# Half-chunk start, split last tile, and DMA transposes with GpSimd norms in a fused FFT and gated-MLP kernel

## The chip, the cores and the metric

The kernel runs on one core of one Trainium2 chip. The metric is device time in microseconds (us) of that core, one number per execution. The kernel before takes 206.59 us (median of the 3 runs that came with it, 204.63 to 207.01).

Engine names are those of the profile: PE (TensorE, matmuls), PEld (its weight loads), DVE (VectorE), ACT (ScalarE), POOL (GpSimd), SP (SyncE, which here only issues DMAs). "SPq" is the issuing of DMAs from SP. Each run has a state. For one core it is called slow when the run is over 1.5% above the fastest of the same kernel, and all ratios use fast runs.

## The reference, cut to what matters

```python
xn = _layernorm(x, axis=-1)                      # x: [1, 2048, 512] bf16
return x + _A_ref(xn, A_w_r, A_w_i) + _B_ref(xn, B_w_gate, B_w_up, B_w_down)

# _A_ref: rfft2 over (2048, 512), times a complex weight, irfft2
# _B_ref: h = gelu(xn @ w_gate) * (xn @ w_up);  h @ w_down     (512 -> 1792 -> 512)
```

## The kernel before

The 2048 rows are 16 tiles of 128, and four tiles are a chunk. Each chunk is normalised, transposed (xnT, features on partitions) and used twice. The MLP takes it in 14 blocks per chunk, each a gate and an up group of four matmuls. The FFT takes it through a "butterfly" (sums and differences) and then units D and A, whose results go out to DRAM and come back transposed as `tv`. Units B and C, a second trip through DRAM (`vv`), and units E and F follow.

Each engine gets one list of instructions, and in the traces an engine that waited at one of them stood idle (DVE for 8.52 us and PE for 8.62 us in the changed kernel). The MLP blocks fill PE, and the FFT units are placed between them by hooks: one hook after each gate, one after each up, three in each down tile. `at(h, ...)` puts work at hook h.

```python
def ln_norm(j):
    op("dve", lambda e: e.tensor_scalar(xn[:, j % 4, :], x_sb[:, j, :], ag[:, j, 0:1], rstd[:, j:j + 1], ALU.subtract, ALU.mult), ...)

def trans(m, dcs, jjs, eng="dve"):               # 8 PE transposes into one PSUM bank, then a copy
    ...
            ins = e.transpose(bank_h(bk)[:, i * P:(i + 1) * P], xn[:, jj, dc * P:(dc + 1) * P], ident[:])
    ...
        op("dve", lambda e: e.tensor_copy(dst, src), r=[("ps", bk)], w=ks)

# the plan (cut): chunks 1 to 3
for m in range(1, 4):
    a = 10 * (m - 1)
    for i in range(4):
        at(a + i, (ln_stat, 4 * m + i))
    at(a + 3, (ln_aggr, 4 * m, 4))
    for i in range(4):
        at(a + 6 + i // 2, (ln_norm, 4 * m + i))
    at(a + 8, (trans, m, (0, 1), (0, 1, 2, 3)))
    at(a + 9, (trans, m, (2, 3), (0, 1, 2, 3)))
    at(a + 10, (butter, m, 0))
    at(a + 11, (butter, m, 1))
...                                              # D of tile 4 at hook 12, of tile 8 at 22, of tile 12 at 32
for i in range(0, 16, 2):
    at(47 + 3 * i, (unit_B, i), (unit_B, i + 1)) # needs all of tv
    at(52 + 3 * i, (unit_C, i), (unit_C, i + 1))
...
# the start (cut): statistics, norms and transposes of all four tiles of chunk 0, then
for b in range(4):
    for fc in range(NFC):
        gate(b, fc); hook(False); up(b, fc); flush(); hook()
        if b > 0 and fc in (2, 5, 8, 11):
            down(b - 1, (fc - 2) // 3)
for jj in range(4):
    down(3, jj)
```

Loads of x, constants and the gate and up weights go out on the SP queue at the start, in order of need. The down weights (wd) and the FFT's weights (Wr, Wi, cm) are issued from POOL at hooks.

## Time and profile before

| what | value | read from |
|---|---|---|
| span of the profiled execution | 205.1 us | the page |
| PE busy | 190.8 us, 93% | the page, part 1 |
| first MLP matmul | 10.69 us | timeline |
| PE idle for tv ahead of the first unit B | 3.85 us | waits, timeline |
| PE idle ahead of transposes, for norms | 1.9 us in 5 waits | waits |
| last DVE add to the end | 201.37 to 205.1 us | timeline |

Three parts of the page follow, cut. First the busy times by engine (busy us, share of the span, instructions). Then the busy tenths of PE in 40 slices of 5.1 us, the granted clock (the share of the full TensorE clock that the chip let PE have) in tenths, and the DMA engines' busy share.

```profile
PE 190.8 (93%) x1131; PEld 93.2 (45%) x1145; DVE 112.1 (55%) x262; ACT 88.3 (43%) x157; POOL 25.9 (13%) x52
...
PE   7898989899999569999999999989999999999992
...
PEclk9999999999999957999999999999999999999999
DMA  5999998626675601556654223230011111111102
```

PE is the engine to look at. Its one large hole lies near 72 us, and the granted clock falls there (0.50 from 72.5 to 79.3 us). The DMA engines are at nine tenths or more from 5 to 31 us.

The chain of waits, in order of time (start us, us, what), shows that hole:

```profile
62.80 4.18 DMA scr<-tt
66.98 0.02 issue
67.00 6.27 DMA tv<-scr
73.27 0.24 issue
73.51 1.07 PE ps L455 x8
74.58 1.82 PE ps L576 x4
```

The last store of unit A and the last reload of tv take 10.5 us together. PE has MLP work for only part of that. After the hole, the four gate matmuls of one block take 1.82 us; elsewhere they take 0.86.

The waits of PE (engine, line, for whom: us in total, times, longest):

```profile
PE ps L455 <- DMA tv<-scr: 3.9, 1, 3.9
PE ps L366 <- DVE xn L356: 1.9, 5, 0.7
PE ps L406 <- DVE arena L392: 1.2, 2, 0.7
```

L366 are the transposes, and L406 is the first matmul of unit D, which waits for the butterfly on DVE.

### The profile page before, as it was taken

How to read it: one execution, taken by the hardware profiler on the slowest of the kernel's cores; microseconds unless marked ns; L12 is line 12 of the kernel's file. 1: busy time of each engine (PE TensorE's matmuls, PEld its weight loads, DVE VectorE, ACT ScalarE, POOL GpSimd, SP SyncE). 2: the span in 40 equal slices, each digit the busy share in tenths (PEclk: the TensorE clock that was granted, in tenths of full speed). 3: DMA queues.
4: the chain of work that ended last, by engine and by line, in shares of the span. 5: the costliest groups of instructions: out<-in, count | busy, mean ns of one | idle time of the engine just before them, and what ended most of it. 6: DMA issues, size and time to landing. Idle time of an engine off the chain costs nothing.

```text
span 205.1 us, 3107 instructions
## 1 busy us (share of the span) xinstructions
PE 190.8 (93%) x1131; PEld 93.2 (45%) x1145; DVE 112.1 (55%) x262; ACT 88.3 (43%) x157; POOL 25.9 (13%) x52
## 2 busy tenths in 40 slices
PE   7898989899999569999999999989999999999992
PEld 3344544445544223444444444435555555555540
DVE  2897786978422233546773677233555454546341
ACT  2135565554553131563545534414636363635210
POOL 0201125031201202222310000000100001010000
PEclk9999999999999957999999999999999999999999
DMA  5999998626675601556654223230011111111102
GB/s 147 221 312 348 281 316 185 197 79 150 107 180 148 120 18 54 113 131 134 157 162 118 62 77 106 69 87 1 16 46 44 36 33 50 39 27 29 26 26 51
DMA packets 19007, 23.09 MB, mean 113 GB/s; under 512 B 2208, under 2 KB 16672, under 8 KB 18608
## 3 DMA queue, kind: packets, MB, share of 16 engines
q1 hardware_dynamic: 16512, 16.79, 30.4%
q0 software_dynamic: 1712, 5.32, 11.8%
q10 hardware_dynamic: 768, 0.79, 1.6%
q8 instruction: 9, 0.15, 0.3%
q14 instruction: 6, 0.05, 0.1%
HBM read 16.57 MB, written 6.31 MB: 112 GB/s over the span
## 4 chain that ended last, share of the span: by engine, by line
PE 73%; DMA 10%; DVE 10%; issue 2%; POOL 1%; ACT 1%; SPq 0%
PE ps L602 20%; PE ps L589 20%; PE ps L576 19%; DMA tv<-scr 3%; DVE hT L592 3%; DVE st L344 3%; PE ps L455 2%; PE ps L481 2%; DMA scr<-tt 2%; DMA scr<-vp 2%; PE ps L515 2%; DMA x_sb<-in_A_x_dram 2%; DMA arena<-scr 2%; DVE xn L356 2%; PE ps L366 1%
## 5 line engine op out<-in xcount | busy, mean ns | idle before, releaser
L592 DVE TENSOR_TENSOR hT<-ps,gl 128x512 bf16<-128x512 f32 x56 | 38.5, 690 | 41.8 <-PE ps L589 36.8
L576 PE MATMUL ps<-xnT,wg 128*128 128x512 f16 x224 | 59.2, 388 | 0.8 <-ACT xnT L378 0.8
L589 PE MATMUL ps<-xnT,wu 128*128 128x512 f16 x224 | 58.4, 384 | 0.0
L579 ACT ACTIVATE gl<-ps 128x512 bf16<-128x512 f32 x56 | 33.4, 597 | 48.1 <-PE ps L576 44.9
L602 PE MATMUL ps<-wd,hT 128*128 128x512 bf16 x210 | 49.8, 379 | 0.8 <-issue 0.2
L576 PEld LDWEIGHTS ps<-xnT,wg 128*128 128x128 bf16 x224 | 21.0, 99 | 24.5 <-issue 4.8
L602 PEld LDWEIGHTS ps<-wd,hT 128*128 128x128 bf16 x224 | 21.3, 98 | 23.2 <-issue 1.0
L589 PEld LDWEIGHTS ps<-xnT,wu 128*128 128x128 bf16 x224 | 21.3, 99 | 22.2 <-issue 2.6
L523 POOL COPY zt<-xn 1x128 bf16<-1x128 bf16 x16 | 4.5, 283 | 79.4 <-ACT zt L522 79.4
L615 DVE TENSOR_TENSOR x_sb<-ps,x_sb 128x512 bf16<-128x512 f32 x11 | 7.6, 690 | 12.0 <-PE ps L602 12.0
L522 ACT ACTIVATE zt<-ps 128x512 bf16<-128x512 f32 x16 | 9.5, 595 | 10.5 <-PE ps L515 10.5
L549 ACT ACTIVATE eo<-ps 128x512 bf16<-128x512 f32 x16 | 9.5, 595 | 9.4 <-PE ps L544 9.4
L487 ACT ACTIVATE vp<-ps 128x514 bf16<-128x514 f32 x16 | 8.7, 598 | 10.1 <-PE ps L481 10.1
L344 DVE BATCH_NORM_STATS2 st<-x_sb 128x6 f32<-128x512 bf16 x16 | 10.6, 685 | 3.6 <-DMA x_sb<-in_A_x_dram 3.6
L413 ACT ACTIVATE xs<-ps 128x512 f16<-128x512 f32 x16 | 9.5, 596 | 6.7 <-PE ps L409 6.6
L461 ACT ACTIVATE xc<-ps 128x514 f16<-128x514 f32 x16 | 8.7, 600 | 6.9 <-PE ps L455 6.9
L440 ACT ACTIVATE tt<-ps 128x514 f16<-128x514 f32 x16 | 8.7, 598 | 3.7 <-PE ps L434 3.1
L554 DVE TENSOR_TENSOR ys<-eo 128x256 bf16<-128x256 bf16 x16 | 4.6, 289 | 9.3 <-ACT eo L549 9.3
L455 PE MATMUL ps<-tv,be 128*64 128x257 f16 x64 | 5.5, 297 | 3.9 <-DMA tv<-scr 3.9
L467 DVE TENSOR_TENSOR m_0<-xc,Wr 128x514 bf16<-128x514 f16 x8 | 3.4, 430 | 10.3 <-ACT xc L461 10.3
L352 POOL TENSOR_TENSOR rstd<-vpe,mhalf 128x4 f32<-128x4 f32 (+1 forms) x5 | 4.6, 918 | 26.6 <-DVE vpe L351 26.6
L338 PE MATMUL ps<-dumm 128*128 128x512 f16 x24 | 6.8, 454 | 1.2 <-DVE dumm L309 1.2
(65 smaller groups left out, 167.2 us busy)
## 6 DMA issues: line engine op xcount, KB each, us to landing
scr<-tt SPq DMA_DIRECT2D x16, 128.5 KB
tv<-scr SPq DMA_DIRECT2D x16, 128.5 KB
scr<-vp SPq DMA_DIRECT2D x16, 128.5 KB
arena<-scr SPq DMA_DIRECT2D x16, 128.5 KB
out_dram<-osb SPq DMA_DIRECT2D x32, 64.0 KB
wg<-in_B_w_gate_dram SPq DMA_DIRECT2D x3, 512.0 KB, 11.2
wu<-in_B_w_up_dram SPq DMA_DIRECT2D x3, 512.0 KB, 13.0
x_sb<-in_A_x_dram SPq DMA_DIRECT2D x5, 256.0 KB, 11.4
```

Source lines behind the costliest of these rows:

```text
L344: op("dve", lambda e: e.bn_stats(st[:, j, :], x_sb[:, j, :]), r=[("x", j, 0), ("x", j, 1)], w=[("st", j)])
L413: op("act", lambda e: e.activation(x4[:].rearrange("p (a c r) -> p a c r", a=2, r=4), bank(bk).rearrange("p (a r c) -> p a c r", a=2, r=4) ...
L440: op("act", lambda e: e.activation(t4[:], pair(bk), ACT.Copy, scale=SC_A), r=[("ps", bk), ("ps", bk + 1)], w=[("tt", j % 4)])
L455: ins = e.matmul(bank(bk + ri)[64 * hh:64 * hh + 64, 0:257], be[:, 64 * ri:64 * ri + 64], tv[:, 16 * hh + h, :], start=True, stop=True, sk ...
L461: op("act", lambda e: e.activation(xc[s2][:, :, 0:KD], pair(bk), ACT.Copy, scale=SC_B), r=[("ps", bk), ("ps", bk + 1)], w=[("xc", s2)])
L522: op("act", lambda e: e.activation(z[:], bank(bk).rearrange("p (a c) -> p a c", a=4), ACT.Copy, scale=SC_E), r=[("ps", bk)], w=[zk])
L549: op("act", lambda e: e.activation(o2[:], bank(bk), ACT.Copy), r=[("ps", bk)], w=[ok])
L576: ins = e.matmul(bank(bg), wg_sb[:, dc, fc * P:(fc + 1) * P], xnT[:, dc, b * 512:(b + 1) * 512], start=(dc == 0), stop=(dc == 3))
L579: op("act", lambda e: e.activation(gl[k % 2][:], bank(bg), ACT.Gelu_apprx_tanh), r=[("ps", bg)], w=[("gl", k % 2)])
L589: ins = e.matmul(bank(bu), wu_sb[:, dc, fc * P:(fc + 1) * P], xnT[:, dc, b * 512:(b + 1) * 512], start=(dc == 0), stop=(dc == 3))
L592: op("dve", lambda e: e.tensor_tensor(hT[b % 2][:, fc, :], bank(bu), gl[k % 2][:], ALU.mult), r=[("ps", bu), ("gl", k % 2)], w=[("hT", b % ...
L602: ins = e.matmul(bank(bk), hT[b % 2][:, fc, jj * P:(jj + 1) * P], wd_sb[:, fc, :], start=(fc == 0), stop=(fc == NFC - 1))
```

## The change

The change has three intents. The first three MLP blocks start on the first half of chunk 0, so that PE begins earlier. The last down tile is finished in two column halves, to shorten the tail. For chunks 1 to 3, the PE transposes and their DVE copies become one DMA transpose each, and half of their norms move to POOL, to relieve PE and DVE. Hooks shift by a few places, there are three gelu buffers and four `zt` buffers, and xnT has another layout. The core of the diff, cut:

```diff
-        load_w(wg_sb, wgv, "wg", 0, 2, "act")
-        load_w(wu_sb, wuv, "wu", 0, 2, "sp")
+        load_w(wg_sb, wgv, "wg", 0, 3, "act")
+        load_w(wu_sb, wuv, "wu", 0, 3, "sp")
 ...
         def ln_norm(j):
-            op("dve", lambda e: e.tensor_scalar(xn[:, j % 4, :], ...
+            eng = "pool" if j >= 4 and j % 2 else "dve"
+            op(eng, lambda e: e.tensor_scalar(xn[:, j % 4, :], ...
 ...
+        def trans_dma(m):
+            op("sp", lambda e: e.dma_start_transpose(xnT[:, 4 * m:4 * m + 4].rearrange("p j a c -> p (j a) c"), xn[:].rearrange("p j d -> p (j d)")),
+               r=[("xn", jj) for jj in range(4)], w=[("xnT", m, dc, jj) for dc in range(4) for jj in range(4)], dma=True)
 ...
+        def last_down(bk):          # two halves of 256 columns, each added and stored by itself,
+            ...                     # its two stores issued from sp and act
 ...
-            a = 10 * (m - 1)
+            a = 9 * (m - 1) + 3
 ...
-                at(a + 6 + i // 2, (ln_norm, 4 * m + i))
-            at(a + 8, (trans, m, (0, 1), (0, 1, 2, 3)))
-            at(a + 9, (trans, m, (2, 3), (0, 1, 2, 3)))
-            at(a + 10, (butter, m, 0))
-            at(a + 11, (butter, m, 1))
+                at(a + 5 + i // 2, (ln_norm, 4 * m + i))
+            at(a + 7, (trans_dma, m))
+            at(a + 11, (butter, m, 0))
+            at(a + 12, (butter, m, 1))
 ...                                # D of tile 4 now at hook 17, of tile 8 at 26, of tile 12 at 35
-            at(47 + 3 * i, (unit_B, i), (unit_B, i + 1))
+            at(49 + 3 * i, (unit_B, i), (unit_B, i + 1))
 ...
+        for fc in range(2):         # before the second half of chunk 0 is transposed
+            gate(0, fc, (0, 1))
+            up(0, fc, (0, 1), fc == 1)
 ...
+        gate(0, 2, (0, 1))
+        up(0, 2, (0, 1))
+                jjs = (2, 3) if b == 0 and fc < 3 else (0, 1, 2, 3)
```

More of the change, by code (lines that the diff above doesn't have):

```diff
@@ L228, in bass_parallel_sum__spectral_gfnet__glu_gated_geglu__prompt_kernel @@
         xn = sb("xn", [P, 4, D], F16)
-        xnT = sb("xnT", [P, 4, S], F16)
+        xnT = sb("xnT", [P, NJ, 4, P], F16)
         arena = sb("arena", [P, 9216], F16)
@@ L255, in bass_parallel_sum__spectral_gfnet__glu_gated_geglu__prompt_kernel @@
         vp = [sb("vp%d" % i, [P, 2, KD], BF16) for i in range(4)]
-        NZ = 6
+        NZ = 4
         zt = [sb("zt%d" % i, [P, 4, P], BF16) for i in range(NZ)]
@@ L259, in bass_parallel_sum__spectral_gfnet__glu_gated_geglu__prompt_kernel @@
         z256 = xn[:].rearrange("p a d -> p (a d)").bitcast(BF16)
-        gl = [sb("gl%d" % i, [P, 512], BF16) for i in range(2)]
+        gl = [sb("gl%d" % i, [P, 512], BF16) for i in range(3)]
         eo = [sb("eo%d" % i, [P, 512], BF16) for i in range(2)]
@@ L320, in bass_parallel_sum__spectral_gfnet__glu_gated_geglu__prompt_kernel @@
         dma("sp", fd[:], c_fd.ap(), w=["fd"])
-        load_w(wg_sb, wgv, "wg", 2, 6, "sp")
-        load_w(wu_sb, wuv, "wu", 2, 6, "sp")
+        load_w(wg_sb, wgv, "wg", 3, 6, "sp")
+        load_w(wu_sb, wuv, "wu", 3, 6, "sp")
         load_x(8, 4, 0, "sp")
@@ L355, in ln_norm @@
         def ln_norm(j):
-            op("dve", lambda e: e.tensor_scalar(xn[:, j % 4, :], x_sb[:, j, :], ag[:, j, 0:1], rstd[:, j:j + 1], ALU.subtract, ALU.mult),
+            eng = "pool" if j >= 4 and j % 2 else "dve"
+            op(eng, lambda e: e.tensor_scalar(xn[:, j % 4, :], x_sb[:, j, :], ag[:, j, 0:1], rstd[:, j:j + 1], ALU.subtract, ALU.mult),
                r=[("x", j, 0), ("x", j, 1), ("ag", j), ("rstd", j)], w=[("xn", j % 4)])
@@ L369, in trans @@
             w = len(jjs) * P
-            c0 = m * 512 + jjs[0] * P
             n = len(dcs)
-            dst = xnT[:, dcs[0]:dcs[0] + n, c0:c0 + w]
-            src = bank_h(bk)[:, 0:n * w].rearrange("p (a c) -> p a c", a=n)
+            j0 = 4 * m + jjs[0]
+            dst = xnT[:, j0:j0 + len(jjs), dcs[0]:dcs[0] + n, :].rearrange("p j a c -> p a j c")
+            src = bank_h(bk)[:, 0:n * w].rearrange("p (a j c) -> p a j c", a=n, j=len(jjs))
             ks = [("xnT", m, dc, jj) for dc in dcs for jj in jjs]
@@ L385, in butter, with t @@
             k = ("fold", m % 2)
-            sl = slice(m * 512, (m + 1) * 512)
+            lo, hi = (xnT[:, 4 * m:4 * m + 4, i:i + 2, :].rearrange("p j a c -> p a j c") for i in (0, 2))
+            def t(ap):
+                return ap.rearrange("p a (j c) -> p a j c", j=4)
             if part == 0:
-                op("dve", lambda e: e.tensor_tensor(ev1, xnT[:, 0:2, sl], xnT[:, 2:4, sl], ALU.add), r=xk(m), w=["ev1"])
-                op("dve", lambda e: e.tensor_tensor(f[:, 2:4, :], xnT[:, 0:2, sl], xnT[:, 2:4, sl], ALU.subtract), r=xk(m), w=[k + (2,), k + (3,)])
+                op("dve", lambda e: e.tensor_tensor(t(ev1), lo, hi, ALU.add), r=xk(m), w=["ev1"])
+                op("dve", lambda e: e.tensor_tensor(t(f[:, 2:4, :]), lo, hi, ALU.subtract), r=xk(m), w=[k + (2,), k + (3,)])
             else:
@@ L567, in bass_parallel_sum__spectral_gfnet__glu_gated_geglu__prompt_kernel, with gate @@
         gun = [0]
-        def gate(b, fc):
+        def gate(b, fc, jjs=(0, 1, 2, 3)):
             k = gun[0]
-            bg = take(1, 0.87, 1.2)
+            n = len(jjs) * P
+            c0 = 4 * b + jjs[0]
+            bg = take(1, 0.0017 * n, 1.2)
             def fn(e):
@@ L575, in fn, with up @@
                 for dc in range(4):
-                    ins = e.matmul(bank(bg), wg_sb[:, dc, fc * P:(fc + 1) * P], xnT[:, dc, b * 512:(b + 1) * 512], start=(dc == 0), stop=(dc == 3))
+                    ins = e.matmul(bank(bg)[:, 0:n], wg_sb[:, dc, fc * P:(fc + 1) * P], xnT[:, c0:c0 + len(jjs), dc, :], start=(dc == 0), stop=(dc == 3))
                 return ins
-            op("pe", fn, r=[("wg", fc)] + xk(b), w=[("ps", bg)])
-            op("act", lambda e: e.activation(gl[k % 2][:], bank(bg), ACT.Gelu_apprx_tanh), r=[("ps", bg)], w=[("gl", k % 2)])
-        def up(b, fc):
+            op("pe", fn, r=[("wg", fc)] + [("xnT", b, dc, jj) for dc in range(4) for jj in jjs], w=[("ps", bg)])
+            op("act", lambda e: e.activation(gl[k % 3][:, 0:n], bank(bg)[:, 0:n], ACT.Gelu_apprx_tanh), r=[("ps", bg)], w=[("gl", k % 3)])
+        def up(b, fc, jjs=(0, 1, 2, 3), wait=False):
             k = gun[0]
             gun[0] += 1
-            bu = take(1, 0.87, 1.8)
+            n = len(jjs) * P
+            c0 = 4 * b + jjs[0]
+            bu = take(1, 0.0017 * n, 1.8)
             def fn(e):
@@ L588, in fn, with mult @@
                 for dc in range(4):
-                    ins = e.matmul(bank(bu), wu_sb[:, dc, fc * P:(fc + 1) * P], xnT[:, dc, b * 512:(b + 1) * 512], start=(dc == 0), stop=(dc == 3))
+                    ins = e.matmul(bank(bu)[:, 0:n], wu_sb[:, dc, fc * P:(fc + 1) * P], xnT[:, c0:c0 + len(jjs), dc, :], start=(dc == 0), stop=(dc == 3))
                 return ins
-            op("pe", fn, r=[("wu", fc)] + xk(b), w=[("ps", bu)])
-            op("dve", lambda e: e.tensor_tensor(hT[b % 2][:, fc, :], bank(bu), gl[k % 2][:], ALU.mult), r=[("ps", bu), ("gl", k % 2)], w=[("hT", b % 2, fc)])
+            op("pe", fn, r=[("wu", fc)] + [("xnT", b, dc, jj) for dc in range(4) for jj in jjs], w=[("ps", bu)])
+            h0 = jjs[0] * P
+            def mult():
+                op("dve", lambda e: e.tensor_tensor(hT[b % 2][:, fc, h0:h0 + n], bank(bu)[:, 0:n], gl[k % 3][:, 0:n], ALU.mult),
+                   r=[("ps", bu), ("gl", k % 3)], w=[("hT", b % 2, fc, jj) for jj in jjs])
+            if wait:
+                later.append(mult)
+            else:
+                mult()
+        def last_down(bk):
+            for c in range(2):
+                cs = slice(256 * c, 256 * c + 256)
+                bc = (bk + c) % 8
+                def fn(e, cs=cs, bc=bc):
+                    ins = None
+                    for fc in range(NFC):
+                        ins = e.matmul(bank(bc)[:, 0:256], hT[1][:, fc, 3 * P:4 * P], wd_sb[:, fc, cs], start=(fc == 0), stop=(fc == NFC - 1))
+                    return ins
+                op("pe", fn, r=[("wd", fc) for fc in range(NFC)] + [("hT", 1, fc, 3) for fc in range(NFC)], w=[("ps", bc)])
+                k = osb_n[0] % 3
+                osb_n[0] += 1
+                op("dve", lambda e, cs=cs, bc=bc, k=k: e.tensor_tensor(osb[k][:, cs], bank(bc)[:, 0:256], x_sb[:, NJ - 1, cs], ALU.add),
+                   r=[("ps", bc), ("acc", NJ - 1)], w=[("osb", k)])
+                for b, eng in ((0, "sp"), (1, "act")):
+                    dma(eng, ov[b, :, NJ - 1, cs], osb[k][64 * b:64 * b + 64, cs], r=[("osb", k)], w=[("out", NJ - 1, b, c)])
+            for _ in range(3):
+                hook()
         def down(b, jj):
@@ L604, in part @@
                 pt[0] += 0.217 * (f1 - f0)
-                op("pe", fn, r=[("wd", fc) for fc in range(f0, f1)] + [("hT", b % 2, fc) for fc in range(f0, f1)], w=[("ps", bk)])
+                op("pe", fn, r=[("wd", fc) for fc in range(f0, f1)] + [("hT", b % 2, fc, jj) for fc in range(f0, f1)], w=[("ps", bk)])
+            if j == NJ - 1:
+                return last_down(bk)
             part(0, 5)
@@ L659, in bass_parallel_sum__spectral_gfnet__glu_gated_geglu__prompt_kernel @@
             for i in range(4):
-                at(a + 6 + i // 2, (ln_norm, 4 * m + i))
-            at(a + 8, (trans, m, (0, 1), (0, 1, 2, 3)))
-            at(a + 9, (trans, m, (2, 3), (0, 1, 2, 3)))
-            at(a + 10, (butter, m, 0))
-            at(a + 11, (butter, m, 1))
-        at(0, (butter, 0, 0))
-        at(1, (butter, 0, 1))
+                at(a + 5 + i // 2, (ln_norm, 4 * m + i))
+            at(a + 7, (trans_dma, m))
+            at(a + 11, (butter, m, 0))
+            at(a + 12, (butter, m, 1))
+        at(2, (butter, 0, 0))
+        at(3, (butter, 0, 1))
         for j in range(NJ):
-            h = (4, 6, 8, 10, 12, 14, 17, 19, 22, 24, 27, 29, 32, 33, 34, 36)[j]
+            h = (8, 10, 12, 14, 17, 19, 21, 23, 26, 28, 30, 32, 35, 36, 37, 38)[j]
             at(h, (unit_D, j))
@@ L672, in bass_parallel_sum__spectral_gfnet__glu_gated_geglu__prompt_kernel @@
         for i in range(0, 16, 2):
-            at(47 + 3 * i, (unit_B, i), (unit_B, i + 1))
-            at(52 + 3 * i, (unit_C, i), (unit_C, i + 1))
-        at(103, (unit_row,))
+            at(49 + 3 * i, (unit_B, i), (unit_B, i + 1))
+            at(54 + 3 * i, (unit_C, i), (unit_C, i + 1))
+        at(105, (unit_row,))
         for j in range(NJ):
-            at(104 + 3 * j, (unit_E, j))
-            at(108 + 3 * j, (unit_F, j))
+            at(106 + 3 * j, (unit_E, j))
+            at(110 + 3 * j, (unit_F, j))
         warm(24)
-        for i in range(2):
-            ln_stat(2 * i)
-            ln_stat(2 * i + 1)
-            ln_aggr(2 * i, 2)
-        for i in range(2):
-            ln_norm(2 * i)
-            ln_norm(2 * i + 1)
-        for i in range(2):
-            trans(0, (0, 1), (2 * i, 2 * i + 1), "dve")
-            trans(0, (2, 3), (2 * i, 2 * i + 1), "act")
+        ln_stat(0)
+        ln_stat(1)
+        ln_aggr(0, 2)
+        ln_stat(2)
+        ln_norm(0)
+        ln_norm(1)
+        ln_stat(3)
+        trans(0, (0, 1), (0, 1), "dve")
+        trans(0, (2, 3), (0, 1), "act")
+        ln_aggr(2, 2)
+        ln_norm(2)
+        ln_norm(3)
+        for fc in range(2):
+            gate(0, fc, (0, 1))
+            up(0, fc, (0, 1), fc == 1)
+        trans(0, (0, 1), (2, 3), "dve")
+        trans(0, (2, 3), (2, 3), "act")
+        flush()
+        gate(0, 2, (0, 1))
+        up(0, 2, (0, 1))
         for b in range(4):
             for fc in range(NFC):
-                gate(b, fc)
+                jjs = (2, 3) if b == 0 and fc < 3 else (0, 1, 2, 3)
+                gate(b, fc, jjs)
                 hook(False)
-                up(b, fc)
+                up(b, fc, jjs)
                 flush()
@@ L702, in bass_parallel_sum__spectral_gfnet__glu_gated_geglu__prompt_kernel @@
         assert not plan
-        pr.wait_all_dma("sp", [pr.writer[("out", j, b)] for j in range(NJ) for b in range(2)])
+        pr.wait_all_dma("sp", [ev for k, ev in pr.writer.items() if k[0] == "out"])
         with nc.Block() as block:
```

## The prediction

> **What bounds the kernel.** TensorE. By the page PE is busy 190.8 of 205.1 us, and 73% of the chain of waits. Chain and timeline show these losses:
>
> - Start: the first MLP matmul runs at 10.69 us, behind both halves' statistics, norms and transposes.
> - 15 to 50 us: PE transposes of chunks 1 to 3, six groups of 8 at about 0.55 us each (3.3 us), plus about 1.3 us of PE idling for VectorE norms in front of them.
> - 69.7 to 73.5 us: PE idles 3.85 us for the last reload of the FFT intermediate from DRAM (tv). Until 79.2 us it then runs at a granted clock of 0.5, which costs about 2.8 us more.
> - Tail: the last VectorE add starts at 201.37 us, takes 0.69, and its stores end the span 3.0 us after it.
>
> **What the change does.**
>
> 1. Half-chunk start. The gate now needs only x tiles 0 and 1. From the durations in the trace (rstd at 6.8, two norms 0.8, transposes 0.6, copy 0.6) I estimate the first gate at about 9.0 to 9.4 us. The up weights' first piece, which landed at 8.5, is 1.5 times as large now, so the first up may wait a few tenths. Gain 1.3 to 1.7 us.
> 2. DMA transposes. They remove 3.3 us of PE, the 1.3 us of waits, 4.1 us of VectorE copies (6 of 0.69) and 2.4 us of VectorE norms (6 of 0.41, now on GpSimd). They add three 512 KB transfers on the SP queue. [...]
> 3. Last tile in column halves: the final add about 0.36 instead of 0.69 us, and its stores split over two issuing queues. Gain about 0.8 us.
>
> **How much is on the critical path.** Items 1 and 3 wholly, together about 2.3 us. Item 2's 4.6 us are too, but something comes back. The page shows the DMA share at 1.0 or more from 4 to 32 us. In the packet times the SP queue works in order, and weight packets occupy it until about 28 us. The first transpose, issued near 20 us, therefore moves only behind them and lands at about 28 to 31 us. The butterfly behind it blocks VectorE, and unit D of tile 4 (wanted by PE near 28 us) comes late: a stall of 1 to 4 us. The tv wait stays, perhaps up to 1 us longer, because the last A units are packed closer.
>
> Sum: -1.5 - 4.6 - 0.8 + 1.8 (stall at D4) + 0.3 (tv) = -4.8 us; from 206.6 that is 201.8, range 197.8 to 205.8. Chances: faster by over 2% (under 202.5) 0.57, within 2% 0.38, slower 0.05.
>
> **What would show it.** First gate near 9.2 us; no transposes on PE after 13 us; SP issue of the first transpose near 20 us; a PE wait at D of tile 4 on VectorE (arena) of 1 to 4 us; a tv wait of 3.5 to 5 us, again with a clock near 0.5; about 2.9 us from the last add's start to the end.
>
> **What would make it wrong.** Transposes much slower [...], which stall D4 past 4 us and drop the clock again (towards 206); or landing early, without a stall, or a tv wait short enough to keep the full clock (towards 197).

## The result, and the profile after

| | runs | median us | range |
|---|---|---|---|
| before | 4 | 206.8 | 204.63 to 207.14 |
| changed | 4 | 225.02 | 223.19 to 227.26 |

One of the four runs of the changed kernel (227.26) counts as slow. The ratio is 1.0876 (95% interval 1.073 to 1.102): the changed kernel is slower by almost 9%. A ratio here is the mean time of one kernel's fast runs over that of the other's of the same rounds, so it is not quite the ratio of the medians. The profiled execution of the changed kernel was fast, with a span of 221.3 us: 16.2 us more than before.

The same parts of the page, after:

```profile
PE 193.9 (88%) x1135; PEld 96.4 (44%) x1135; DVE 107.2 (48%) x254; ACT 88.4 (40%) x160; POOL 38.7 (17%) x58
...
PE   7699950896991999299999999999899999999993
...
PEclk9979996599997699889999999999999999999999
DMA  5999989338279147314566532224002111211011
```

DVE has become lighter, as intended, by 4.9 us. But PE now has four deep holes in the first 100 us, and the clock is low in four places. From about 100 us on, little differs.

The waits of PE, after:

```profile
PE ps L414 <- DVE arena L400: 15.6, 3, 8.6
PE ps L463 <- DMA tv<-scr: 4.2, 1, 4.2
...
PE ps L601 <- DMA wu<-in_B_w_up_dram: 0.6, 1, 0.6
PE ps L367 <- DMA ident<-c_id: 0.5, 1, 0.5
```

L414 is the old L406: unit D of tiles 4, 8 and 12, one wait per chunk. It grew from 1.2 to 15.6 us. The wait for tv (L463) grew only from 3.9 to 4.2. The timeline shows the first of these waits (start us, us, engine, line, operation, out<-in, count, and in brackets the idle time before it and for whom):

```profile
23.32 4.28 POOL L357 TENSOR_SCALAR xn<-x_sb,ag,rstd 128x512 f16<-128x512 bf16 x2
...
27.69 1.93 SPq L382 DMA_TRANSPOSE xnT<-xn  x1
...
36.36 0.69 DVE L396 TENSOR_TENSOR arena<-xnT 128x1024 f16<-128x1024 f16 x1 [8.52 <-DMA xnT<-xn]
...
39.57 0.29 PE L414 MATMUL ps<-fd,arena 128*128 128x128 f16 x1 [8.62 <-DVE arena L400]
```

The two POOL norms run one after the other until 27.60 us; DVE had finished its two by 24.59. The transpose is issued only then and lands at 36.34. DVE waits 8.52 us for it, and PE 8.62 for DVE. The chain of waits shows the three transposes from issue to landing:

```profile
27.69 8.65 DMA xnT<-xn
...
47.53 4.28 DMA xnT<-xn
...
61.54 7.02 DMA xnT<-xn
```

A look at three stretches around the first stall (stretch: us, busy us of PE, PEld, DVE, ACT and POOL with instructions, clock, DMA share, GB/s) gives the second cost:

```profile
34.00:39.50 5.50, 0.00 (x0) 0.00 (x0) 3.14 (x7) 0.00 (x0) 0.00 (x0) 0.56 1.08 284
39.50:45.00 5.50, 5.43 (x18) 2.52 (x19) 3.48 (x11) 1.71 (x3) 4.26 (x4) 0.51 0.31 93
45.00:47.00 2.00, 2.00 (x16) 0.86 (x15) 0.50 (x1) 0.85 (x3) 1.95 (x2) 1.00 0.15 39
```

After the idle time PE works 5.4 us at half clock, which loses about 2.7 us more. After the third stall (71.0 to 75.5 us, PE busy 4.3 us at clock 0.50) it loses about 2.1. The short second stall, 1.7 us, costs no clock.

The start, which was to be the sure gain, went the other way. Before, the first gate was:

```profile
10.69 1.02 PE L576 MATMUL ps<-xnT,wg 128*128 128x512 f16 x4 [0.78 <-ACT xnT L378]
```

After:

```profile
9.73 0.60 PE L586 MATMUL ps<-xnT,wg 128*128 128x256 f16 x4 [0.78 <-ACT xnT L379]
10.91 1.03 PE L601 MATMUL ps<-xnT,wu 128*128 128x256 f16 x4 [0.58 <-DMA wu<-in_B_w_up_dram]
11.73 1.06 PE L586 MATMUL ps<-xnT,wg 128*128 128x256 f16 x4
12.59 1.06 PE L601 MATMUL ps<-xnT,wu 128*128 128x256 f16 x4
13.44 0.97 PE L367 MATMUL ps<-ident,xn 128*128 128x128 f16 x8
```

The first gate runs 1.0 us earlier than before, but the first up waits for its weights until 10.9 us. The half blocks that follow take 0.85 us from start to start instead of 0.43, at a granted clock of 0.50, until about 14 us. The gate of the fourth block starts at 17.80 us; before it was 16.20, with one unit D already done.

The tail is the time from the last VectorE add to the end of the span. Before, and then after:

```profile
201.37 0.69 DVE L615 TENSOR_TENSOR osb<-ps,x_sb 128x512 bf16<-128x512 f32 x1 [2.33 <-PE ps L602]
...
218.01 0.42 DVE L628 TENSOR_TENSOR osb<-ps,x_sb 128x256 bf16<-128x256 f32 x1 [1.10 <-PE ps L623]
```

So the 16.2 us of the two traces add up about like this (differences of the waits, and half-clock time worked out as busy time times the missing part of the clock):

| term | us |
|---|---|
| waits ahead of units D: 15.6 - 1.2 | +14.4 |
| half clock after the stalls, at the start and after tv: about 7.8 - 2.8 | +5.0 |
| wait of the first up, and 0.3 more for tv | +0.9 |
| PE transposes and waits for norms saved | -4.6 |
| tail, last add's start to the end 3.73 to 3.29 us | -0.4 |
| sum | +15.3 |

About 1 us is left without a name.

### The profile page after: what moved, and what is told of

Its sections match the earlier page's. It is cut to its first block, busy times and chain, and to the rows that moved or that the text cites. A ratio compares the mean times of both kernels' runs of the same rounds, so it can differ in the third digit from the quotient of the medians.

```text
span 221.3 us, 3097 instructions
## 1 busy us (share of the span) xinstructions
PE 193.9 (88%) x1135; PEld 96.4 (44%) x1135; DVE 107.2 (48%) x254; ACT 88.4 (40%) x160; POOL 38.7 (17%) x58
## 2 busy tenths in 40 slices
DMA packets 25407, 24.66 MB, mean 111 GB/s; under 512 B 8480, under 2 KB 23072, under 8 KB 25008
## 4 chain that ended last, share of the span: by engine, by line
PE 70%; DMA 21%; DVE 5%; issue 1%; SPq 1%; ACT 0%
PE ps L586 20%; PE ps L601 18%; PE ps L643 17%; DMA xnT<-xn 9%; DMA wu<-in_B_w_up_dram 4%; DMA tv<-scr 3%; PE ps L463 2%; PE ps L489 2%; DMA scr<-vp 2%; DMA scr<-tt 2%; PE ps L523 2%; DMA arena<-scr 2%; PE ps L623 1%; DVE hT L607 1%; DVE st L344 1%
## 5 line engine op out<-in xcount | busy, mean ns | idle before, releaser
L586 PE MATMUL ps<-xnT,wg 128*128 128x512 f16 (+1 forms) x236 | 61.4, 385 | 1.1 <-ACT xnT L379 0.8
L607 DVE TENSOR_TENSOR hT<-ps,gl 128x512 bf16<-128x512 f32 (+1 forms) x59 | 39.0, 663 | 47.4 <-PE ps L601 42.1
L601 PE MATMUL ps<-xnT,wu 128*128 128x512 f16 (+1 forms) x236 | 60.1, 379 | 0.6 <-DMA wu<-in_B_w_up_dram 0.6
L589 ACT ACTIVATE gl<-ps 128x512 bf16<-128x512 f32 (+1 forms) x59 | 34.0, 576 | 53.5 <-PE ps L586 51.9
L586 PEld LDWEIGHTS ps<-xnT,wg 128*128 128x128 bf16 x236 | 22.8, 102 | 24.8 <-issue 5.1
L601 PEld LDWEIGHTS ps<-xnT,wu 128*128 128x128 bf16 x236 | 23.0, 101 | 23.2 <-issue 2.9
L414 PE MATMUL ps<-fd,arena 128*128 128x128 f16 x16 | 3.9, 243 | 15.6 <-DVE arena L400 15.6
L357 POOL TENSOR_SCALAR xn<-x_sb,ag,rstd 128x512 f16<-128x512 bf16 x6 | 12.7, 2118 | 0.3
L396 DVE TENSOR_TENSOR arena<-xnT 128x1024 f16<-128x1024 f16 x4 | 2.8, 690 | 17.2 <-DMA xnT<-xn 17.2
L414 PEld LDWEIGHTS ps<-fd,arena 128*128 128x128 f16 x16 | 1.7, 108 | 19.4 <-DVE arena L400 17.1
```

The source lines that it names most:

```text
L357: op(eng, lambda e: e.tensor_scalar(xn[:, j % 4, :], x_sb[:, j, :], ag[:, j, 0:1], rstd[:, j:j + 1], ALU.subtract, ALU.mult), r=[("x", j, ...
L586: ins = e.matmul(bank(bg)[:, 0:n], wg_sb[:, dc, fc * P:(fc + 1) * P], xnT[:, c0:c0 + len(jjs), dc, :], start=(dc == 0), stop=(dc == 3))
L589: op("act", lambda e: e.activation(gl[k % 3][:, 0:n], bank(bg)[:, 0:n], ACT.Gelu_apprx_tanh), r=[("ps", bg)], w=[("gl", k % 3)])
L601: ins = e.matmul(bank(bu)[:, 0:n], wu_sb[:, dc, fc * P:(fc + 1) * P], xnT[:, c0:c0 + len(jjs), dc, :], start=(dc == 0), stop=(dc == 3))
L607: op("dve", lambda e: e.tensor_tensor(hT[b % 2][:, fc, h0:h0 + n], bank(bu)[:, 0:n], gl[k % 3][:, 0:n], ALU.mult), r=[("ps", bu), ("gl", k ...
```

## The experiments

Fifteen kernels ran. "Before" was run again, and each ratio is against it.

### Undoing one part of the change at a time

**Norms back on VectorE.**

```diff
-            eng = "pool" if j >= 4 and j % 2 else "dve"
+            eng = "dve"
```

> The changed kernel, with all norms back on VectorE (each 0.41 us there, 2.1 us on GpSimd). Theory A (GpSimd norms and DMA transposes both delay the butterflies; each is a share of the three stalls): the first transpose is issued near 24.7 us in place of 27.7, the PE stall at D of tile 4 falls from 8.6 to about 5 to 6 us, the later ones by 2 to 3 us, total about 8 us less (near 217). Theory B (the DMA transpose alone makes the stalls, because its transfer waits for the queue): under 3 us less. Theory C (the GpSimd norms alone make them): the stalls vanish and the time is under 207.

Measured: ratio 1.0816 (interval 1.078 to 1.085), median 223.39 us of 6 runs, 218.59 to 224.52. Only two of the six were within 1.5% of the fastest, so the ratio rests on those two, and most runs were close to the changed kernel's time. The chain of waits:

```profile
23.83 16.62 DMA xnT<-xn
```

The transpose was issued 3.9 us earlier and landed 4.1 us later, at 40.45 us. My reading, for which no packets of this run are shown, is this: issued earlier, it stood longer behind the weight loads of its own queue and ran beside more of the down-weight loads, which GpSimd could issue earlier without norms to do first (in the changed kernel its first three come at 27.55 us, right behind the norms). The stalls ahead of D are 15.7 us in all, as in the changed kernel. Theory A expected 8 us less and is wrong in this part: with the norms alone undone, almost nothing comes back.

**PE transposes back, norms still half on GpSimd.**

```diff
-            at(a + 7, (trans_dma, m))
+            at(a + 7, (trans, m, (0, 1), (0, 1, 2, 3)))
+            at(a + 8, (trans, m, (2, 3), (0, 1, 2, 3)))
```

> The changed kernel with the PE transposes back in place of the DMA transposes, norms still half on GpSimd. Theory A: PE now waits for the GpSimd norms at its transposes, 2 to 3 us each time, without the DMA's 4 to 9 us; about 10 us less than the change (near 214 to 216). Theory B (DMA alone): at or below 208. Theory C (GpSimd norms alone): still 222 or more.

Measured: ratio 1.0979 (interval 1.094 to 1.102). Three runs lie between 226.5 and 227.73 us. The fourth, which carried the profile, took 1,107 us with its matmuls about four times as long (those of L601 1,634 ns in the mean, in the changed kernel 379). It is not used, so this kernel has no usable trace. The DMA transposes alone are not the cause either: without them the kernel is as slow as with them. Taken alone, the first run would have pointed to the DMA transposes (theory B) and this one to the GpSimd norms (theory C).

**Both undone.** The edits are the two above together.

> The changed kernel with both undone: PE transposes and VectorE norms, but the half-chunk start, the last tile in halves and the shifted hooks stay. Theory A, B and C all say near the kernel before, 205 to 209. Rival D (the shifted hooks or the half-chunk start make much of the loss): 211 or more.

Measured: ratio 1.023 (1.017 to 1.029), median 211.6 us. Together the two undone parts bring back about 13 of the 18 us, though each alone brings back almost nothing. What is left is the half-chunk start and the moved hooks (and the new xnT layout, whose copies and butterflies take 0.68 to 0.69 us as before). Its trace shows PE waiting 5.8 us for VectorE norms ahead of the transposes and 1.9 us for the first up weights. The median is just inside rival D (211 or more), though two of the four runs are under 211.

**The start of before, all else as changed.** Pieces of two blocks, chunk 0 whole.

> The changed kernel with the start of before (whole chunk 0 first, weight pieces of 2 blocks), all else as changed. If the half-chunk start loses, as the trace suggests (first up waits for its weights until 10.9 us and PE then runs at clock 0.5 until 14 us, fourth block at 17.8 against 16.2 us): the fourth block starts about 1.5 us earlier; but the stall at D of tile 4 waits on the transpose behind the weights, so only 0 to 1.5 us of it may reach the end. If the half-chunk start helps, as predicted: 1 to 2 us slower.

Measured: ratio 1.1211 (1.117 to 1.126), 231.63 us: about 7 us slower than the changed kernel by the two ratios. In the trace the first transpose takes 17.7 us from issue (25.03) to landing, against 8.65. With the earlier pace it was issued sooner (25.03 against 27.69 us), by my reading while more of the weight loads were still in flight; in the changed kernel the last of their packets on its own queue ends at 28.6 us. The question about the start itself was not answered by this kernel, because the transposes answer louder.

### Each part alone, on the kernel before

Undoing parts gave effects that do not add. So each part was put alone on the kernel before. (The half start and the DMA transposes bring the changed kernel's xnT layout and its gelu and `zt` buffers with them; these were not tested apart.)

**The split last tile alone.** `last_down` is added to the kernel before, and nothing else.

> The kernel before with the last down tile in column halves alone. As predicted: about 0.8 us faster (ratio 0.996). Rival: no gain, because the stores of the tiles ahead of it hold the queue: ratio 0.999 to 1.001.

Measured: ratio 0.9904 (0.985 to 0.996), 205.2 us: faster, by 0.9 us or more. In the trace the last add starts at 201.09 us and the span ends at 204.1, which is 3.0 us; before it was 3.73. This part is good, for about 0.7 us. More of the measured gain may be the clock: in this trace the half clock lasts about 3.4 us (an estimate from its mean clock, 0.992 of 204.1 us), before 6.8, and the mean clock of the fast runs is 0.991 to 1.000, before 0.983 to 0.991. Nothing shows that the edit caused that.

**The half-chunk start alone.** The start, pieces of three blocks, three gelu buffers, all hooks two later.

> The kernel before with the half-chunk start alone (weight pieces of three blocks, three gelu buffers, hooks two later, PE transposes, VectorE norms at the old distances). As I predicted: 1.3 to 1.7 us faster. After the trace of the changed kernel: the first up waits for its larger weight piece and PE falls to half clock for 3 us, so 0 to 4 us slower.

Measured: ratio 1.0111 (1.006 to 1.016), 209.28 us: about 2.3 us slower.

**The DMA transposes alone.** Norms on VectorE, hooks and start of before.

```diff
-            at(a + 8, (trans, m, (0, 1), (0, 1, 2, 3)))
-            at(a + 9, (trans, m, (2, 3), (0, 1, 2, 3)))
+            at(a + 8, (trans_dma, m))
```

> The kernel before with the DMA transposes alone, in the hooks of before and with all norms on VectorE. The transpose of chunk 1 is issued about 20 us, in the middle of the weight loads. If its latency is set by the transfers that share the engines: it lands only near 35 us or later (12 us or more after the issue), PE stalls over 10 us, and the kernel is 12 us or more slower. If a DMA transpose costs its 4 us wherever it is issued: under 5 us slower.

Measured: ratio 1.1425 (1.135 to 1.150), 236.0 and 236.6 us in the two fast runs: 29 us slower. The profiled execution was a slow one (245.18 us), so its times are only a hint. There the first transpose was issued at 20.91 us and landed 23.9 us later. A fast trace of nearly the same kernel follows below.

**The GpSimd norms alone.** Only the one-line choice of the engine.

> The kernel before with half the norms of chunks 1 to 3 on GpSimd alone. If the two slow GpSimd norms (2.1 us each, in series) delay the PE transposes as they delayed the DMA ones: 3 stalls of 2 to 4 us each, 6 to 15 us slower with the clock drops. If there is slack for them: under 2 us.

Measured: ratio 1.0527 (1.048 to 1.058), 217.56 us: 11 us slower. In its trace:

```profile
18.66 4.27 POOL L357 TENSOR_SCALAR xn<-x_sb,ag,rstd 128x512 f16<-128x512 bf16 x2
...
23.08 1.01 PE L367 MATMUL ps<-ident,xn 128*128 128x128 f16 x8 [3.05 <-POOL xn L357]
```

PE waits about 3 us for POOL at each of the three chunks (8.8 us in all), and the clock falls again at the first and third of these waits (3.05 and 2.60 us; not at the second, of 3.15: the next four up matmuls take 0.88 us there, and 1.71 behind the third). One norm takes 2.07 us on POOL and 0.41 on DVE.

So of the four parts one helps a little, the half start costs a little, the GpSimd norms cost 5%, and the DMA transposes alone cost 14%. The changed kernel lost less than the last two together. The slow norms are not enough to explain this, since with VectorE norms it still lost only 8.2%. Its hooks also leave more time: unit D follows a transpose by seven hooks there, and by four in the kernel with the DMA transposes alone. This lead was not tested by itself.

### What makes a DMA transpose slow

The page counts 8,480 DMA packets under 512 bytes after, and 2,208 before. 6,144 of these 6,272 more are the transposes: the packet records of the trace show 2,048 packets of 256 bytes for each. While the first one runs, from 29.0 to 34.5 us, the down-weight loads of the POOL queue send 144 packets of 4,096 bytes at the same time; the packets of the second one, with little beside them, take 2.6 us. The test is to hold those loads back.

```diff
+        def load_wd(dst, src, keys):
+            op("pool", lambda e: e.dma_start(dst, src), w=keys, dma=True, after=[("pe", pr.cnt["pe"]), pr.writer[("xnT", 1, 0, 0)]])
 ...
-            at(10 + 2 * i, (load_late, wd_sb[:, f0:f1, :], ...))
+            at(11 + 2 * i, (load_wd, wd_sb[:, f0:f1, :], ...))
```

> The changed kernel, with the down-weight loads of the GpSimd queue held until the transpose of chunk 1 has landed. Theory E (a transpose is 2,048 packets of 256 bytes, and large packets of the other queue in flight with it slow it): issue to landing of chunk 1 falls from 8.65 us to about 4.3 us, the value of the undisturbed one of chunk 2, the stall at D of tile 4 from 8.6 to about 4.3 us; 4 to 6 us faster than the change (217 to 219). Rival F (the SP queue's own backlog or a fixed cost): no change, 222 or more.

Measured: ratio 1.057 (1.051 to 1.063), 218.25 us, as theory E had it. Chunk 1 in the chain:

```profile
26.11 4.89 DMA xnT<-xn
```

It takes 4.89 us in place of 8.65, and the PE stall at D of tile 4 is 4.2 in place of 8.6 us. All stalls ahead of D together fall from 15.6 to 10.5 us:

```profile
PE ps L417 <- DVE arena L403: 10.5, 3, 4.2
```

Theory E does not cover the third transpose, which takes 7.0 us in the changed kernel and 7.1 here. In the changed kernel its packets run in 2.8 us, nearly as fast as those of the undisturbed one (2.6), but the first comes 1.9 us after the issue (1.2 in the undisturbed one), and the landing 2.2 us or more after the last (0.5). Why was not tested.

The same hold was put on the kernel with the DMA transposes alone (there the loads stay at hook 10).

> The kernel with the DMA transposes alone (VectorE norms, hooks of before), with the same hold on the down-weight loads. Theory E: the transpose issued at 20.9 us still has to follow the weight loads of its own queue until 28 us, but then runs alone: landing near 30 us in place of 44.8, and the kernel 10 to 18 us faster than the one without the hold (221 to 229). Rival F: landing still after 40 us.

Measured: ratio 1.1134 (1.107 to 1.120), 230.72 us, about 6 us better than without the hold. Theory E had the landing right (near 30 us), but not the time: it expected 10 to 18 us. The fast trace points to another condition. The transpose is issued at 20.50 us, behind the weight loads of its own queue (the last two at 16.76 and 17.39); its issue keeps SP for 7.78 us (1.93 for the first one in the changed kernel), and it lands at 30.3. All stalls ahead of D are still 22.5 us.

Last, three things that had stood in front of the transposes or beside them were removed together: VectorE norms, the hold, and the first group of Wr, Wi and cm loads moved from hook 26 to hook 30, behind the third transpose.

> The changed kernel with all three DMA transposes, but with VectorE norms, the down-weight loads held behind the first transpose, and the first Wr/Wi/cm group four hooks later, behind the third. If late norms and company are the whole cause: the transposes land in 4.3 us (chunks 2 and 3), the stalls together fall from 15.6 us to under 5 us, and the time is 208 to 212. If the lead of four hooks is too short even then: stalls of 2 to 4 us at each chunk remain and the time is 213 to 217.

Measured: ratio 1.0348 (1.028 to 1.042), 213.51 us: the second reading by its time. The stalls ahead of D are 7.9 us in all, but uneven (5.0, 1.3 and 1.6):

```profile
PE ps L417 <- DVE arena L403: 7.9, 3, 5.0
```

The three transposes:

```profile
23.52 7.86 DMA xnT<-xn
38.27 8.40 DMA xnT<-xn
53.50 6.26 DMA xnT<-xn
```

The first still follows its own queue's weight loads (the last two issued at 17.04 and 17.67 us), and its issue keeps SP for 5.08 us. The second, as I read it, meets the down weights that were held back until the first landed (31.4 us); no packets of this run are shown for it. Against the run with VectorE norms alone (16.6 us for a first transpose issued 0.3 us later), the first is 8.8 us shorter: that is what holding back the down weights is worth here. Quiet moments for the DMA engines are rare in this kernel (before, their share is 0.75 or more from 2 to 38 us), and by this reading a load that is moved away from one transpose meets another.

### The clock, the start, and a version that beats both

**Is the fall of the clock a consequence of idle time?** On the kernel before, the wait for tv was partly filled with dummy matmuls.

```diff
+        at(47, (fill, 14))       # 14 matmuls on a zeroed tile, into a free PSUM bank
         for i in range(0, 16, 2):
             at(47 + 3 * i, (unit_B, i), (unit_B, i + 1))
```

> The kernel before, with 14 dummy matmuls (3.0 us) in the idle time of TensorE ahead of the first unit B. If the fall of the granted clock to 0.5 follows from that idle time and costs 2.8 us: 2 to 3 us faster (ratio 0.986 to 0.990), and no half clock from 73 to 79 us. If the clock falls for another reason: no gain, or up to 1 us slower.

Measured: ratio 0.9896 (0.985 to 0.995), 204.44 us. In its trace PE idles 0.8 us for tv, and the clock stays at 1.00 from 70 to 80 us. The stretch behind the wait, in the kernel before and then with the fill (clock third from the end):

```profile
73.00:79.00 6.00, 5.49 (x19) 2.27 (x20) 3.13 (x9) 1.69 (x3) 0.61 (x1) 0.50 0.09 22
...
75.00:80.00 5.00, 5.00 (x30) 2.20 (x29) 3.31 (x10) 2.09 (x5) 1.80 (x3) 1.00 0.29 80
```

So the half clock behind this wait follows from its idle time, and the useless matmuls made the kernel about 2 us faster.

**The half-chunk start with small weight pieces.** First pieces of two blocks, two half blocks instead of three.

> The kernel before with the half-chunk start alone, as the earlier run with it, but with first weight pieces of two blocks and two half blocks in place of three. If the larger piece made the loss: the first up waits under 0.3 us, the clock stays at 1.0 from 11 to 14 us, and the kernel is 0 to 1.5 us faster than before (the run with pieces of three was 2.3 us slower). If the half-chunk start loses as such: still 1.5 to 3 us slower.

Measured: ratio 1.0122 (1.008 to 1.017), 208.98 us: no better than the one with large pieces. The clock now stays at 1.00 from 8 to 18 us, so half blocks ran without it here. That the larger piece causes the half clock is not shown: by an estimate from their mean clocks, three traces with that piece (VectorE norms back, 0.961; the hold, 0.960; the hold with VectorE norms, 0.967) also keep the full clock at the start, since the stretches behind their stalls account for what is lost. But the third block's up then waits for its weights until 15.65 us, and the fourth gate runs at 16.52, later than the 16.20 of the kernel before. In this trace that wait takes back what PE gained by being ready sooner. The 2 us of loss are only in part accounted for: 0.3 us at the fourth gate, with a unit D (0.3 us) still to do, and a wait for tv of 4.7 us in place of 3.9. The rest was not settled.

**MLP work in the wait for tv.** Built on the split last tile: units B and C start five hooks later and are packed closer, so that the end of the chain stays where it was. Two groups of the FFT's weights are loaded later too.

```diff
-            at(47 + 3 * i, (unit_B, i), (unit_B, i + 1))
-            at(52 + 3 * i, (unit_C, i), (unit_C, i + 1))
+            at(52 + 2.64 * i, (unit_B, i), (unit_B, i + 1))
+            at(57 + 2.64 * i, (unit_C, i), (unit_C, i + 1))
-        for i, h0 in enumerate((26, 42, 52, 62)):
+        for i, h0 in enumerate((26, 46, 54, 62)):
```

> A version meant to beat both: the kernel before, the last tile in halves, and units B and C started five hooks later and packed closer (2.64 in place of 3 hooks for each), so that MLP work fills the wait for tv. If all of the idle 3.9 us and the half clock of 2.8 us go and the end of the chain is not later: 6 to 7 us faster by it and 1 to 2 us by the tail, ratio 0.96 to 0.97. If the wait only moves behind the last unit C: ratio 0.98 to 1.0.

Measured: ratio 0.9743 (0.970 to 0.979), 201.19 us: 2.6% faster than before and the best kernel. The page's PE and clock rows have no hole left:

```profile
PE   7988989999999999999999999999999999999993
...
PEclk9999999999999999999999999999999999999999
```

It did not reach the 0.96 to 0.97 that was expected for it.

**DMA transposes with a longer lead.** On top of the respaced kernel, DMA transposes for chunks 2 and 3 only, VectorE norms, the butterfly five hooks after the issue. (Units D, B and C, and one group of the FFT's weights, also stand at other hooks than in the respaced kernel, so the difference is not the transposes' alone.)

> The respaced kernel with DMA transposes for chunks 2 and 3 alone, VectorE norms, and the butterfly five hooks (4.3 us and more) after the issue in place of two to four. If the lead hides the transposes, it gains the 2.2 us of PE transposes and some VectorE waits: ratio 0.960 to 0.968 (the respaced one had 0.974). If not: 0.975 to 1.0, with PE waits at D of tiles 8 and 12.

Measured: ratio 0.996 (0.991 to 1.001), 205.69 us, worse than the respaced kernel without them. The transpose of chunk 2 took 8.2 us among the FFT's own stores and reloads, and PE waited 4.9 us for it. Even five hooks of lead do not cover that.

## Why the prediction was wrong, point by point

I predicted 201.8 us, range 197.8 to 205.8; the changed kernel takes 225.02.

- **The step that failed** is the sentence "the first transpose, issued near 20 us, therefore moves only behind them and lands at about 28 to 31 us", with "a stall of 1 to 4 us" at D of tile 4 alone, entered in the sum as +1.8. Measured: issued at 27.69, landed at 36.34, PE stalls of 8.6, 1.7 and 5.3 us at all three chunks, 15.6 in all. The mechanism (late xnT, butterfly, D) was right. Its size in the sum was wrong by a factor of eight (14.4 us more than before, against 1.8), and two of the three places were missing. The issue was late because the transpose waited for two GpSimd norms in series (until 27.60).
- **The GpSimd norms were entered as a pure saving** ("2.4 us of VectorE norms (6 of 0.41, now on GpSimd)"), and no cost stood against it. They cost 2.1 us each and run in series in front of a transpose. Alone they make the kernel 5.3% slower. I read what the move took off DVE and not that the butterfly, PE and the whole chunk wait for the slower of the two engines.
- **The transpose's own time** was a figure that no trace had shown, and too short. In the quietest case here its 512 KB move in 2.6 us of packets (about 200 GB/s), and it takes 4.3 us from issue to landing. In company it takes 6 to 18 in fast executions. I had named much slower transposes as a danger, but gave it too little of the range.
- **Chunks 2 and 3 have no term in the sum.** The second transpose ran undisturbed and still took 4.3 us, and PE stalled for 1.7. The third, beside loads of Wr and FFT stores, took 7.0, and PE stalled for 5.3.
- **The clock.** I counted its loss for the tv wait and did not carry it over to the new stalls. The two longer stalls lost 2.7 and 2.1 us more. The filled kernel shows for the tv wait that the cause is the idle time (0.8 us in place of 3.85, and a clock of 1.00). In the two kernels the clock fell 2.8 to 4.0 us after PE went idle (at 34.65 us after 30.95, for one), not after an idle time of 1.7 us, and it came back 3.2 to 5.8 us after PE resumed. Its changes in the changed kernel (10.76, 14.17, 34.65, 44.89, 68.79, 75.61, 92.68 and 96.09 us) lie 3.41, 20.48, 10.24, 23.89, 6.83, 17.07 and 3.41 us apart, in this one trace all whole multiples of 3.41. The length of a wait alone did not decide: an idle time of 1.87 us was followed by half clock (start of the kernel with both undone), one of 3.15 us was not (GpSimd norms alone). At the start of the changed kernel the clock fell at 10.76 us although no gap but the 1.2 us ahead of the first matmul was over 0.8; in the 3 us before it PE was busy for 1.3.
- **The half-chunk start** was "gain 1.3 to 1.7 us", with "a few tenths" for the weights. Measured alone, it loses 2.3 us. The first gate came earlier, at 9.73 (I had 9.0 to 9.4), but PE then waits for weights, and with the larger first piece it ran for 3 us at half clock.
- **Right:** the direction of the tail (I had 0.8 us; 0.4 in this trace, 0.7 in that of the tail alone), the tv wait of 3.5 to 5 us (4.2), again with a low clock, and no PE transposes after the start.
- **The parts do not add.** Undoing either GpSimd norms or DMA transposes returned nothing, and undoing both returned 13 us. My reading is that with two causes in series in front of one wait, either is enough to make PE late; for the kernel with GpSimd norms and PE transposes there is no usable trace to show it. And the slow norms, as I read it, had kept the first transpose away from part of the weight loads: without them it landed 4.1 us later.

## What to carry to other kernels

When work moves to a slower or an asynchronous engine, cost the latency on the path to the next consumer, not the busy time that it takes off the old engine. Ask where in time the new transfer falls and what is in flight with it. Where undoing single parts returns nothing, try each part alone and both together before naming a cause. A wait on TensorE can cost more than itself through the clock (here those of 8.6, 5.3, 4.2, 3.85, 3.05, 2.60 and 1.87 us did, those of 3.15 and 1.7 us did not), so look first for a wait that useful work can fill: here that, with the split last tile, made the kernel 2.6% faster.
